# Row maxima sent through memory: as single values, or turned on VectorE and sent in 128-byte pieces

## The chip, the cores and the metric

The kernel runs on one core of one Trainium2 chip. The metric is the time of one execution on the device in microseconds (us), the slowest core's; here there is one. The core has TensorE (PE) for matmuls, VectorE (DVE), ScalarE (ACT) and GpSimd (POOL) for the rest, SyncE (SP) that only issues transfers, and 16 DMA engines that carry them. Each engine takes its instructions in the order in which they stand, and a transfer is issued by an instruction in some engine's order.

## The reference

Four batches of eight heads, 768 positions, 64 dimensions. Each query and key gets six hash bits (the signs of its products with six random vectors); a query sees only the keys of the same bucket. The attention's output goes through a feed-forward layer with a gate that is a convolution over three positions.

```python
q_bits = (np.einsum('bhsd,dk->bhsk', q, proj) > 0)
k_bits = (np.einsum('bhsd,dk->bhsk', k, proj) > 0)
mask = q_bucket[:, :, :, None] == k_bucket[:, :, None, :]
scores = scale * np.matmul(q, k.transpose(0, 1, 3, 2))
scores = np.where(mask, scores, -1000000000.0)
scores = scores - np.max(scores, axis=-1, keepdims=True)
attn = np.exp(scores)
attn = attn / (np.sum(attn, axis=-1, keepdims=True) + 1e-09)
x = np.matmul(attn, v)                  # heads joined: (4, 768, 512)
h = np.maximum(x @ w_in, 0.0)           # 512 -> 1024
gate = 1.0 / (1.0 + np.exp(-conv_out))  # conv_out: h over 3 positions
out = (h * gate) @ w_out                # 1024 -> 512
```

## The kernel before, in words

The order of the work is written out by hand; every engine runs its instructions as the code records them. Two heads make a pair: 16 pairs, four to a batch, and after every fourth pair the feed-forward layer of that batch.

Matmuls take operands that are split into a high and a low part. For a pair, Q and K stand with the dimensions on the partitions: tile q's first half (QA) has the high part in partitions 0 to 63, the hash bits in 64 to 95 as large numbers that make keys of another bucket lose, and **in partition 96 a row with each query's maximum**. The row of K that meets it is -1, so the score matmul (L290) subtracts the maximum, and ScalarE can take the exponential straight from the matmul's result (L293, tile p). Scores stand with the keys on the partitions, so the maximum has to be a row along the queries.

The maxima are made one pair ahead. `peak(t, h)` multiplies 128 queries (tile t of 6) of head h with all 768 keys (L246, tile m), and VectorE reduces that to one value per query (L249), a column of the tile `stat`, which has the 128 queries on the partitions. Such a column has to become a stretch of QA's row 96. For the first pair TensorE does that (`shift_now`). For the other 15 it goes through memory, on ScalarE's queue: `shift_away` writes columns of `stat` to a tile `top` in memory (L269), `shift_back` reads `top` as rows into QA's row 96 (L272). Each of the 15 pairs does it twice: for tiles 0 to 3 (eight columns, two heads) and for tiles 4 and 5 (four columns).

A pair takes six iterations, i = 0 to 5. Each has the scores and exponentials of two key tiles (L290, L291, L293), up to three `peak`s of the next pair, and the value matmuls (L301, tile v, eight a time) of the iteration before. i = 0 to 2 are the first 416 queries, 3 to 5 the other 352. The sums' additions (L316 on POOL, L314 on VectorE), the division (L334 to L345) and the output's split (L349, L353) follow. `shift_away` for tiles 0 to 3 stands in i = 4 behind the first exponential, its `shift_back` ahead of the exponentials of i = 5; for tiles 4 and 5 they stand in i = 0 and i = 1 of the pair that uses them.

Meanwhile the pair after next is prepared, on SyncE's queue: load R (L161, both heads' Q and K) and v (L165); hash R on TensorE (L174, in i = 3); turn the signs to bits on VectorE (L180); write the bits to memory (L183, far<-bits, 192 KB); make the high part on ScalarE (L188, hi) and the low part on POOL (L192, R); move hi and far into place (L198 to L201, each in an early and a late part); then hi and the low part into the second half of q and k (L207), and only then load the next R. SyncE's queue is in order too: k<-far (L199) holds all that stands behind it until far<-bits has landed.

In batch 0 the weights are also split into high and low parts, step by step, on VectorE, ScalarE and POOL (L90 to L112, tiles wu, wl, wi, wo).

Of the kernel before, what the change touches and what calls it, by code (L numbers as in the profile page):

```python
# [7 lines left out]
F32 = mybir.dt.float32  # L8
# [9 lines left out]
P = 128  # L18
NP = H // 2
NCK = S // P  # L20
# [24 lines left out]
def lsh_attention_conv_ffn(ctx, tc, qk, v, hw, w_in, conv_w, w_out, consts, ident_in, out):  # L45
    nc = tc.nc
    PSUM = bass.MemoryType.PSUM
    cp = ctx.enter_context(tc.tile_pool(name="const", bufs=1))
    wp = ctx.enter_context(tc.tile_pool(name="work", bufs=1))
# [4 lines left out]
    def ring(pool, bufs, shape, dtype, tag, name):  # L54

        k = turns[tag] = (turns.get(tag, -1) + 1) % bufs
        return pool.tile(shape, dtype, tag=f"{tag}{k}", name=name, bufs=1)
# [12 lines left out]
    dp = ctx.enter_context(tc.tile_pool(name="dram", bufs=1, space=bass.MemoryType.DRAM))  # L70
# [53 lines left out]
    def fetch(n):  # L124

        for src, name in blocks[:n]:
            raw = cp.tile([P, 2 * WC], I32, tag=f"w{name}", name=f"raw{name}")
            nc.sync.dma_start(raw, src)
            fetched.append((raw, name))
        del blocks[:n]  # L130

    def background(rate, stop):

        step[0] += 1
        if rate and len(fetched) > (2 if blocks else 0) and step[0] // rate > (step[0] - 1) // rate:
            splits.append(split_weight(*fetched.pop(0)))
        now = splits[:]
        while now:
            for g in now[:]:
                ended = next(g, None)  # L140
                if ended is None:
                    splits.remove(g)
                if ended is None or ended >= stop:
                    now.remove(g)


    class Pair:
# [94 lines left out]
        def peak(self, t, h):  # L242

            mp = ring(ps, 3, [P, 2, 512], F32, "S", f"m{self.nm}_{t}_{h}")[:, :, :HS + 2]
            for half in range(2):
                nc.tensor.matmul(mp[:, half], self.QA[:96, h, t * P:(t + 1) * P],  # L246
                                 self.K[0][:96, h, half * HS:(half + 1) * HS + 2], start=True, stop=True)
            c = self.column(t, h)
            nc.vector.tensor_reduce(self.stat[:, c:c + 1], mp, mybir.AxisListType.XY, ALU.max)  # L249
# [4 lines left out]
        def shift_now(self, t0, n):  # L254
# [7 lines left out]
            for h in range(2):  # L262
                nc.scalar.copy(self.QA[96:97, h, t0 * P:(t0 + n) * P], tp[96:97, h, :n * P])

        def shift_away(self, t0, n):
            c = self.column(t0, 0)
            k = turns["E"] = (turns.get("E", -1) + 1) % 4
            self.top = dp.tile([2 * n, P], F32, tag=f"top{k}", name=f"top{self.nm}_{t0}")
            nc.scalar.dma_start(self.top.rearrange("c p -> p c"), self.stat[:, c:c + 2 * n])  # L269

        def shift_back(self, t0, n):
            nc.scalar.dma_start(self.QA[96:97, :, t0 * P:(t0 + n) * P].bitcast(F32),  # L272
                                self.top.rearrange("(h t) p -> h (t p)", h=2).unsqueeze(0))


    class Block:
# [122 lines left out]
    def load_table(func):  # L399

        nc.scalar.activation(spare, cst[:, 3:4], func)
# [59 lines left out]
    first = pairs[0]  # L461
# [11 lines left out]
    def bring(n):  # L473

        if n < len(pairs):
            pairs[n].place_b()
        if n + 1 < len(pairs):
            pairs[n + 1].load()
        if n < len(pairs):
            pairs[n].load_v()  # L480
# [4 lines left out]
    for n, pr in enumerate(pairs):  # L485
        nxt, nx2 = (pairs[n + k] if n + k < len(pairs) else None for k in (1, 2))
        if nxt:
            units += [(nxt, t, h) for t in range(NCK) for h in range(2)]
        if n == 0 or pr.p:
            bring(n + 1)  # L490
        for i in range(6):
            places = (PEAKS if n else PEAKS_0)[i]

            def peak(place):
                if place in places and units:
                    u, t, h = units.pop(0)
                    u.peak(t, h)

            for bk in late:
                bk.divide()  # L500
                tail.append(bk)
            late = []
            ready, waiting = waiting, []
            blk = both[n][i // 3]
            if i == 5 and nxt:
                nxt.shift_back(0, 4)
            if i == 1 and n:
                pr.shift_back(4, 2)
            for k in range(2):
                c = 2 * (i % 3) + k  # L510
                if len(blk.pts) == c:
                    blk.scores(c)
                waiting.append((blk, c))
                if k == 0:
                    if i == 4 and nxt:
                        nxt.shift_away(0, 4)
                    if i == 0 and n:
                        pr.shift_away(4, 2)
                    peak(0)
                    for bk in tail:  # L520
                        bk.out_high()
            peak(1)
            for bk in tail:
                bk.out_low()
            tail = []
            for bk, c in ready:
                bk.values(c)
                if c <= DADD:
                    bk.add(c)
            if n == 0 and i == 2:  # L530
                first.shift_now(4, 2)
            for bk in summing:
                bk.sums()
                bk.invert()
            late, summing = summing, [bk for bk, c in ready if c == NCK - 1]
            background(RATE, 1)
            peak(2)
            if i == 5 and nx2:
                nx2.place_a(slice(0, EARLY_Q), slice(0, EARLY_K))
            for bk, c in ready:  # L540
                if c > DADD:
                    bk.add(c)
            if nx2:
                if i == HASH:
                    nx2.hash()
                    nx2.bits_up()
                    nx2.high()
                if i > HASH:
                    nx2.low(i - HASH - 1)
            if n or i:  # L550
                fetch(1)
            background(RATE, 1)
        if nx2:
            nx2.place_a(slice(EARLY_Q, S), slice(EARLY_K, S))
        if pr.p == NP - 1:
            bk, rest = both[n][1], waiting
            waiting = []
            load_table(AF.Sigmoid)
            bring(n + 2)

            def fill(i, tile):
                if i == 0:
                    for b2, c in rest:
                        b2.add(c)
                if i == 1:
                    for b2, c in rest:
                        b2.values(c)
                if i == 2:
                    bk.sums(tile[:, 0, :])
                    bk.invert()  # L570
                    bk.divide()
                if i == FLAG:
                    bk.out_high()
                    bk.out_low()

            def ahead():
                if nxt:
                    both[n + 1][0].scores(0)

            ffn(pr.b, [pairs[pr.b * NP + c].x for c in range(NCC)], fill, ahead)  # L580
# [42 lines left out]
```

## Time and profile before

| | |
|---|---|
| median of 3 runs | 990.1 us (987.84 to 996.34) |
| the profiled execution's own time | 990.33 us |
| its span, first to last instruction | 988.5 us |
| mean granted TensorE clock | 0.872 of full speed |
| busy, share of the span | PE 79%, DVE 56%, POOL 42%, ACT 36% |
| batches of attention, roughly | 0 to 206, 300 to 460, 533 to 694, 768 to 912 us |
| feed-forward layers, roughly | 206 to 300, 460 to 533, 694 to 768, 912 to 988 us |

Times in the profile are us from the span's start. A line such as "L293 ACT p<-s" names the line of the kernel, the engine, and the tiles written and read. "ACTq" and "SPq" are the queues of those engines, where transfers are issued. In brackets at an instruction's end stands how long its engine was idle before it, and what ended that.

### The profile page before, as it was taken

The page shows a single profiled execution, that of the slowest core. Times are in us where ns is not written, and L with a number is a line of the kernel's source. Part 1 is how long each engine was busy: PE and PEld are TensorE (multiplying, and loading weights), DVE is VectorE, ACT ScalarE, POOL GpSimd, SP SyncE. Part 2 cuts the span into 40 slices and gives each one's busy share as a digit, 9 for nine tenths or more (in the row PEclk, how much of TensorE's full clock was granted, in tenths as well). Part 3 has the DMA queues.
Part 4 walks back from the last instruction along what each step waited for, and adds up shares of the span by engine and source line. Part 5 has one row for each costly group of instructions (what it writes and reads, how often), then busy time and mean ns, then how long its engine had stood idle before and what let it go on. Part 6 is the DMA issues. An engine that isn't in the chain of part 4 may idle for free.

```text
span 988.5 us, 9984 instructions
## 1 busy us (share of the span) xinstructions
PE 784.7 (79%) x3552; PEld 547.5 (55%) x3552; DVE 550.4 (56%) x728; ACT 360.0 (36%) x582; POOL 410.4 (42%) x264
## 2 busy tenths in 40 slices
PE   6757575866896786787997877868999669678998
PEld 4433343445784443445896544534888445345896
DVE  4566676798862452645663535436665346363664
ACT  4324241444452232333543323322555323233553
POOL 5454646565423553533222534435122345334222
PEclk9878777797998897978999878879899889788999
DMA  3765757351005355364204163553500444600000
GB/s 102 199 117 170 126 160 115 89 109 47 0 32 33 51 120 99 69 137 79 80 32 32 14 112 75 117 95 77 145 0 32 33 59 112 114 2 0 1 32 33
DMA packets 57918, 75.48 MB, mean 76 GB/s; under 512 B 27872, under 2 KB 36334, under 8 KB 57868
## 3 DMA queue, kind: packets, MB, share of 16 engines
q1 hardware_dynamic: 33940, 74.60, 36.4%
q10 hardware_dynamic: 23928, 0.24, 1.2%
q8 instruction: 28, 0.46, 0.2%
q14 instruction: 22, 0.18, 0.1%
HBM read 29.71 MB, written 9.33 MB: 39 GB/s over the span
## 4 chain that ended last, share of the span: by engine, by line
PE 43%; DMA 34%; DVE 14%; ACT 4%; issue 3%; SPq 2%; ACTq 1%; DVEq 0%
DMA top<-stat 17%; PE o L389 11%; PE v L301 8%; DMA k<-far 8%; PE spot L364 7%; DMA far<-bits 5%; PE m L246 5%; PE h L364 4%; PE s L290 3%; DVE ht L373 3%; DVE stat L249 3%; PE s L291 3%; DMA q<-top 2%; PE sum L324 1%; DVE ps L314 1%
## 5 line engine op out<-in xcount | busy, mean ns | idle before, releaser
L293 ACT ACTIVATE p<-s 128x836 f32<-128x836 f32 (+1 forms) x192 | 152.6, 811 | 427.8 <-DMA top<-stat 214.3
L249 DVE TENSOR_REDUCE stat<-m 128x1 f32<-128x772 f32 x192 | 181.5, 953 | 175.6 <-PE m L246 174.4
L246 PE MATMUL m<-k,q 96*128 96x386 f32 x384 | 128.4, 419 | 137.7 <-ACT p L293 94.4
L316 POOL TENSOR_TENSOR ps<-ps,p 128x832 f32<-128x832 f32 (+1 forms) x92 | 157.7, 1714 | 187.2 <-ACT p L293 177.9
L246 PEld LDWEIGHTS m<-k,q 96*128 96x128 f32 x384 | 72.8, 219 | 204.2 <-ACT p L293 109.2
L290 PE MATMUL s<-q,k 97*128 97x418 f32 (+1 forms) x384 | 155.3, 405 | 29.8 <-DMA q<-top 19.3
L301 PE MATMUL v<-p,v 128*64 128x418 f32 (+1 forms) x768 | 173.0, 578 | 2.5 <-DVE bits L180 2.5
L381 POOL TENSOR_TENSOR g<-ht,g 128x384 fp32r<-128x384 f32 x64 | 69.3, 1083 | 220.4 <-ACT g L380 196.3
L373 DVE SCALAR_TENSOR_TENSOR ht<-ht,cw 128x384 f32<-128x384 f32 (+1 forms) x128 | 119.7, 935 | 56.6 <-ACT ht L371 53.3
L389 PE MATMUL o<-wo,g 128*128 128x512 f32 x576 | 145.2, 399 | 6.3 <-DVE r L334 6.3
L291 PE MATMUL s<-q,k 128*128 128x418 f32 (+1 forms) x384 | 145.4, 379 | 0.0
L389 PEld LDWEIGHTS o<-wo,g 128*128 128x128 f32 x576 | 108.7, 190 | 28.2 <-DVE r L334 6.6
L290 PEld LDWEIGHTS s<-q,k 97*128 97x128 f32 x384 | 84.5, 220 | 70.8 <-issue 25.3
L316 POOL TENSOR_TENSOR ps<-p,p 128x832 f32<-128x832 f32 (+1 forms) x32 | 58.5, 1828 | 123.4 <-ACT p L293 123.4
L364 PE MATMUL spot<-xh,wi 128*128 128x386 f32 x320 | 92.9, 352 | 11.6 <-ACT ht L369 11.5
L301 PEld LDWEIGHTS v<-p,v 128*64 128x64 f32 x768 | 52.9, 155 | 75.6 <-issue 69.0
L291 PEld LDWEIGHTS s<-q,k 128*128 128x128 f32 x384 | 84.7, 221 | 1.4
L353 DVE TENSOR_TENSOR xl<-r,xh 128x416 fp32r<-128x416 f32 (+1 forms) x32 | 34.6, 1081 | 73.1 <-ACT xh L349 73.1
L376 ACT ACTIVATE ht<-ht 128x384 f32<-128x384 f32 x64 | 33.6, 525 | 106.7 <-DVE ht L373 106.7
L192 POOL TENSOR_TENSOR R<-R,hi 128x768 fp32r<-128x768 f32 x30 | 66.0, 2202 | 14.1 <-PE hash L174 8.2
L364 PEld LDWEIGHTS spot<-xh,wi 128*128 128x128 f32 x320 | 61.1, 195 | 17.5 <-ACT ht L369 14.1
L364 PE MATMUL h<-xh,wi 128*128 128x386 f32 x192 | 56.7, 358 | 0.0
(83 smaller groups left out, 734.4 us busy)
## 6 DMA issues: line engine op xcount, KB each, us to landing
R<-in_qk SPq DMA_DIRECT2D x15, 768.0 KB
v<-in_v SPq DMA_DIRECT2D x16, 384.0 KB
k<-hi SPq DMA_DIRECT2D x16, 384.0 KB
q<-hi SPq DMA_DIRECT2D x16, 384.0 KB
out<-osb SPq DMA_DIRECT2D x24, 256.0 KB
q<-R SPq DMA_DIRECT2D x15, 384.0 KB
k<-R SPq DMA_DIRECT2D x15, 384.0 KB
rawi<-in_w_in SPq DMA_DIRECT2D x8, 512.0 KB
```

The source lines that it names most:

```text
L192: nc.gpsimd.tensor_tensor(R, R.bitcast(F32), self.hi[:, h].bitcast(F32), ALU.subtract)
L246: nc.tensor.matmul(mp[:, half], self.QA[:96, h, t * P:(t + 1) * P], self.K[0][:96, h, half * HS:(half + 1) * HS + 2], start=True, stop=True)
L249: nc.vector.tensor_reduce(self.stat[:, c:c + 1], mp, mybir.AxisListType.XY, ALU.max)
L290: nc.tensor.matmul(sp[:, h], pr.KA[:97, h, ks], pr.Q[0][:97, h, qs], start=True, stop=False)
L291: nc.tensor.matmul(sp[:, h], pr.KB[:, h, ks], pr.Q[1][:, h, qs], start=False, stop=True)
L293: nc.scalar.activation(self.pts[c], sp, AF.Exp, scale=SCALE)
L301: nc.tensor.matmul(self.av[h * D:(h + 1) * D], pr.v[:, c, h, :], self.pts[c][:, h], start=(c == 0), stop=(c == NCK - 1), tile_position=(0, ...
L316: eng.tensor_tensor(self.acc, first if c == 1 else self.acc, pt, ALU.add)
L364: nc.tensor.matmul(hp[:, :HW], w, x[:, c0:c0 + HW], start=(n == 0), stop=(n == 3 * NCC - 1))
L373: nc.vector.scalar_tensor_tensor(t[:, a:z], ht[:, o + k - 1 + a:o + k - 1 + z], cw[:, f, k:k + 1], t[:, a:z], ALU.mult, ALU.add)
L381: nc.gpsimd.tensor_tensor(g[:, 1, :], t, g[:, 0, :].bitcast(F32), ALU.subtract)
L389: nc.tensor.matmul(op, l, r, start=(f == 0 and n == 0), stop=(f == NFC - 1 and n == 2))
```

## The change

A new function `turn` transposes 32 columns of `stat` on VectorE, in 32 x 32 blocks: block a of the result `side` (partitions 32a to 32a + 31) holds in partition 32a + c the values of column c for the queries 32a to 32a + 31. It is called right behind the last `peak` that fills the columns. `shift_away` then writes `side` instead of `stat`: a tile of 32 rows of 128 values in memory, each written as four pieces of 32 values. `shift_back` reads the rows it needs. All 32 columns that are turned are written, also those that nobody reads.

```diff
+        def turn(self, t0):
+            c = self.column(t0, 0)
+            self.side = ring(wp, 2, [P, 32], F32, "side", f"side{self.nm}_{t0}")
+            nc.vector.transpose(self.side, self.stat[:, c:c + 32])
+
         def shift_away(self, t0, n):
-            c = self.column(t0, 0)
             k = turns["E"] = (turns.get("E", -1) + 1) % 4
-            self.top = dp.tile([2 * n, P], F32, tag=f"top{k}", name=f"top{self.nm}_{t0}")
-            nc.scalar.dma_start(self.top.rearrange("c p -> p c"), self.stat[:, c:c + 2 * n])
+            self.top = dp.tile([32, P], F32, tag=f"top{k}", name=f"top{self.nm}_{t0}")
+            nc.scalar.dma_start(self.top.rearrange("c (a q) -> a c q", a=4), self.side)
 
         def shift_back(self, t0, n):
             nc.scalar.dma_start(self.QA[96:97, :, t0 * P:(t0 + n) * P].bitcast(F32),
-                                self.top.rearrange("(h t) p -> h (t p)", h=2).unsqueeze(0))
+                                self.top[:2 * n].rearrange("(h t) p -> h (t p)", h=2).unsqueeze(0))
...
                     u, t, h = units.pop(0)
                     u.peak(t, h)
+                    if h and t in (3, NCK - 1) and u is not first:
+                        u.turn(t // 4 * 4)
```

The order on SyncE, POOL and TensorE is the same as before, and on ScalarE too. VectorE has 30 more instructions. Here is VectorE before, at i = 3 of the last pair of batch 0, where the last two maxima of tile 3 are reduced (m and stat are those of `peak`, ps the sums, bits the hash bits):

```order
L249 TENSOR_REDUCE stat_83<-m_0_3_0_1169 128x1
L98 TENSOR_SCALAR wlo_1108<-wuo_1107 128x512
L100 SCALAR_TENSOR_TENSOR wlo_1108<-rawo_645,wlo_1108 128x512
L249 TENSOR_REDUCE stat_83<-m_0_3_1_1180 128x1
L314 SCALAR_TENSOR_TENSOR ps_3_0_1090<-ps_3_0_1090,p_3_0_5_1129 128x832
L180 TENSOR_SCALAR bits_1_1190<-hash_1_1185,cst 128x384
```

And the same place with the change (the lines behind the new function have moved by four):

```order
L249 TENSOR_REDUCE stat_83<-m_0_3_0_1181 128x1
L98 TENSOR_SCALAR wlo_1120<-wuo_1119 128x512
L100 SCALAR_TENSOR_TENSOR wlo_1120<-rawo_651,wlo_1120 128x512
L249 TENSOR_REDUCE stat_83<-m_0_3_1_1192 128x1
L268 STREAM_TRANSPOSE side_0_0_1196<-stat_83 128x32
L318 SCALAR_TENSOR_TENSOR ps_3_0_1102<-ps_3_0_1102,p_3_0_5_1141 128x832
L180 TENSOR_SCALAR bits_1_1204<-hash_1_1199,cst 128x384
```

The transpose stands between the reduction and the addition to the sums; the hash bits, which SyncE's queue waits for, come two instructions behind it. ScalarE's order at i = 4 and 5 of the same pair, before:

```order
L293 ACTIVATE p_3_1_2_1207<-s_3_1_2_1202 128x2x352
L269 DMA top_0_0_1209<-stat_83 128x8x1
L293 ACTIVATE p_3_1_3_1216<-s_3_1_3_1211 128x2x352
L272 DMA q_0_75<-top_0_0_1209 1x2x512
L293 ACTIVATE p_3_1_4_1258<-s_3_1_4_1253 128x2x352
```

and with the change:

```order
L297 ACTIVATE p_3_1_2_1221<-s_3_1_2_1216 128x2x352
L273 DMA top_0_0_1223<-side_0_0_1196 4x32x32
L297 ACTIVATE p_3_1_3_1230<-s_3_1_3_1225 128x2x352
L276 DMA q_0_75<-top_0_0_1223 1x2x512
L297 ACTIVATE p_3_1_4_1272<-s_3_1_4_1267 128x2x352
```

Nothing has moved here; what the transfer to memory writes is 4 x 32 x 32 values where it was 128 x 8 x 1.

## Rows read from the trace of the kernel before

**Rows 1.** The page, section 4: the chain of work that ended last, by line, as shares of the span.

```profile
DMA top<-stat 17%; PE o L389 11%; PE v L301 8%; DMA k<-far 8%; PE spot L364 7%; DMA far<-bits 5%; PE m L246 5%; PE h L364 4%; PE s L290 3%; DVE ht L373 3%; DVE stat L249 3%; PE s L291 3%; DMA q<-top 2%; PE sum L324 1%; DVE ps L314 1%
```

**Rows 2.** From the list of who waited for whom: us in total, times, longest. Then the transfer's issues: count, shortest, median and longest issue in ns, first and last start in us.

```profile
ACT p L293 <- DMA top<-stat: 214.3, 24, 10.8
...
L269 ACTq DMA_DIRECT2D top<-stat x30: 361/366/415, 49.1 to 887.1; - x30
```

**Rows 3.** TensorE's timeline, 355 to 402 us, the value matmuls alone: start, us, instruction.

```profile
357.29 1.62 PE L301 MATMUL v<-p,v 128*64 128x418 f32 x8
...
361.73 1.62 PE L301 MATMUL v<-p,v 128*64 128x418 f32 x8
...
366.48 1.41 PE L301 MATMUL v<-p,v 128*64 128x352 f32 x8
...
370.95 1.41 PE L301 MATMUL v<-p,v 128*64 128x352 f32 x8
...
382.18 2.60 PE L301 MATMUL v<-p,v 128*64 128x352 f32 x8
...
390.52 2.17 PE L301 MATMUL v<-p,v 128*64 128x418 f32 x8
...
397.23 1.62 PE L301 MATMUL v<-p,v 128*64 128x418 f32 x8
```

**Rows 4.** Windows of the same pair: from and to, length, then busy us (instructions) of PE, weight loads, DVE, ACT and POOL, the granted clock, the DMA engines' share, GB/s.

```profile
357.30:371.00 13.70, 13.64 (x77) 8.03 (x76) 10.49 (x16) 5.35 (x8) 8.98 (x6) 1.00 0.42 109
371.00:390.50 19.50, 10.27 (x37) 6.00 (x36) 4.77 (x5) 3.58 (x5) 5.00 (x3) 0.74 0.54 87
390.50:397.20 6.70, 6.70 (x27) 3.84 (x26) 4.06 (x7) 2.78 (x4) 4.04 (x3) 0.75 0.54 118
```

**Rows 5.** ScalarE's timeline, 355 to 402 us: the transfers to memory (L269) and back (L272), and the exponential behind each transfer back.

```profile
365.67 0.36 ACTq L269 DMA_DIRECT2D top<-stat  x1
...
375.89 0.56 ACTq L272 DMA_DIRECT2D q<-top  x1
376.55 0.76 ACT L293 ACTIVATE p<-s 128x704 f32<-128x704 f32 x1 [9.49 <-DMA top<-stat]
...
380.98 0.37 ACTq L269 DMA_DIRECT2D top<-stat  x1
...
389.85 0.55 ACTq L272 DMA_DIRECT2D q<-top  x1
390.50 1.63 ACT L293 ACTIVATE p<-s 128x836 f32<-128x836 f32 x2 [7.29 <-DMA top<-stat]
```

**Rows 6.** Other transfers that write to memory. Two steps of the chain that ended last (start, us from issue to landing), and SyncE's wait at the program's end for the last output.

```profile
22.64 4.65 DMA far<-bits
...
560.51 11.43 DMA far<-bits
...
SPq L619 <- DMA out<-osb: 2.1, 1, 2.1
```

**Rows 7.** The DMA view. ScalarE's queue, q10, from 365 to 377 us and from 380.9 to 390 us: packets, MB, their time as a share of 16 engines; and SyncE's k<-hi beside far<-bits, in the stretch from 365 to 377 and in that from 22.6 to 27.3.

```profile
q10 hardware_dynamic: 1040, 0.00, 3.9%
...
q10 hardware_dynamic: 528, 0.00, 3.4%
...
k<-hi SPq DMA_DIRECT2D x1, 256.0 KB
...
k<-hi SPq DMA_DIRECT2D x1, 384.0 KB
```

**Rows 8.** VectorE's transposes from the groups by line and shape: count, busy us, mean ns of one, idle before.

```profile
L342 DVE STREAM_TRANSPOSE r<-rec 128x416 f32<-128x416 f32 x16 | 9.6, 597 | 0.0
L342 DVE STREAM_TRANSPOSE r<-rec 128x352 f32<-128x352 f32 x16 | 8.6, 537 | 0.2
```

**Rows 9.** SyncE's queue from 355 to 402 us (start, us of the issue), and TensorE's hash of two pairs.

```profile
363.84 0.85 PE L174 MATMUL hash<-R,hw_sb 128*32 128x384 f32 x8
...
366.40 0.58 SPq L183 DMA_DIRECT2D far<-bits  x1
367.09 0.61 SPq L198 DMA_DIRECT2D k<-hi  x1
377.90 0.81 SPq L199 DMA_DIRECT2D k<-far  x1
...
384.16 0.60 SPq L207 DMA_DIRECT2D k<-hi  x1
...
390.06 0.59 SPq L207 DMA_DIRECT2D k<-R  x1
395.56 0.38 SPq L161 DMA_DIRECT2D R<-in_qk  x1
...
403.76 0.85 PE L174 MATMUL hash<-R,hw_sb 128*32 128x384 f32 x8
```

**Rows 10.** Behind the feed-forward layer of batch 0: ScalarE's transfers, and the matmul at which TensorE stood.

```profile
300.25 0.36 ACTq L269 DMA_DIRECT2D top<-stat  x1
...
311.02 0.57 ACTq L272 DMA_DIRECT2D q<-top  x1
...
312.61 1.01 PE L246 MATMUL m<-k,q 96*128 96x386 f32 x2 [7.28 <-ACT p L293]
```

**Rows 11.** The chain that ended last, at the last pair of batches 1 and 2: start, us.

```profile
446.86 11.21 DMA top<-stat
...
681.88 10.28 DMA top<-stat
```

**Rows 12.** Window of batch 0 from its first transfer of maxima on, columns as in rows 4.

```profile
49.00:206.00 157.00, 106.00 (x452) 61.98 (x451) 111.15 (x138) 48.37 (x71) 88.70 (x52) 0.79 0.59 125
```

## The prediction

> **What bounds the kernel now.** I read the page first. On the chain that ended last the largest entry is no engine but a transfer, top<-stat, with 17% of the span, ahead of every matmul line [rows 1]. The list of waits says who stands still: ScalarE's exponentials (L293) lost 214.3 us in 24 waits, 10.8 us at the longest, put down to that transfer, and the program issues it 30 times [rows 2]. So it stalls ScalarE's queue nearly every time.
>
> Then I looked at one pair in the middle of a batch. The eight value matmuls (L301) of each iteration mark its pace [rows 3]. Four starts from 357.29 on are 4.44, 4.75 and 4.47 us apart; the next intervals are 11.23, 8.34 and 6.71. A pair thus takes 39.9 us, of which 13.7 are even pace and 26.3 are three iterations that would need 13.3. [...]
>
> ScalarE's timeline tells what the stall is [rows 5]. The transfer to memory is issued at 365.67; the transfer back (L272) can leave only when it has landed, at 375.89, 10.2 us later; it stands in ScalarE's queue ahead of the next exponential, which starts at 376.55. The second of the pair, with half the columns, is issued at 380.98 and holds the queue until 389.85, 8.9 us.
>
> **Why it takes so long.** The packets of that queue (q10, which ScalarE feeds) number 1040 and 528 in the two stretches, and fill 3.9% and 3.4% of the engines' time [rows 7]. So the time isn't reading; it is the writing of single values. Half the values take nearly the same time (8.9 against 10.2 us), and after the feed-forward layer the half-size one takes 10.8 [rows 10]. So the count of values alone doesn't set it; 512 single values cost about what 1024 do. Other writes to memory bound it. The last output transfer, long rows, is over 2.1 us after the program's end begins to wait for it [rows 6]. The hash bits, rows of 1536 bytes and 192 KB, land in 4.65 us at 22.64, where no such transfer runs, and in 11.43 us at 560.51, right behind one [rows 6]. So the single values also delay the transfer behind them, and with it SyncE's queue: k<-far waits for those bits from 366.40 to 377.90 [rows 9].
>
> **The change, part by part.** (1) 30 transposes on VectorE. The trace has transposes of 416 and 352 columns at 597 and 537 ns [rows 8]; the slope of 0.94 ns a column puts 32 columns at 0.24 us, bounds 0 and 0.54. VectorE is busy 10.49 of 13.70 us where it is busiest in a pair [rows 4], and the transfer is issued behind an exponential, so I cost the 30 x 0.24 = 7 us at nothing; uncovered, they add 7.
>
> (2) The transfer now has 128 pieces of 128 bytes. Landing: at least 2.1 us (the output row), at most what it takes now, 8.9 to 10.8. Between these I take 3.1: if pieces cost alike, 1040 packets took 10.2 - 2.1 = 8.1 us, so 128 take 1.0, plus 2.1. The nearest row, the bits with as many pieces twelve times as long, lies at 4.65; I keep 2.1 and 6.2 (below, rival A) for the range. The issue itself (0.36 us) stays.
>
> (3) What it frees. Between the issue behind the first exponential of an iteration and the transfer back at the next iteration's start lies about one iteration, 4.45 us. A landing of 3.1 fits, so the wait on ScalarE goes. The broken iterations then run at 4.45: 6.8 + 3.9 + 2.3 = 12.9 us per joint between two pairs at most, and a pair takes 27.0.
>
> (4) What is late next. SyncE's loop [rows 9]: bits issued (366.40), landed 4.65 later, seven issues from 377.90 to 384.16 and two more of about 0.65, 7.6 us; k<-R lands 5.5 after its issue (390.06 to 395.56); the next load of R takes at most until the next hash, 8.2 (395.56 to 403.76); hash to bits 2.56 (363.84 to 366.40). Sum 28.5, near 27.0; the load is likely done earlier. I take 28.0, so 12 us a joint, not 12.9.
>
> The sum against the profiled execution's 990.3 us (span 988.5; the median of the runs, 990.1, is the same):
> - nine joints inside batches 1 to 3: 9 x 12 = 108.
> - three first pairs behind a feed-forward layer: TensorE idle 7.28 us there [rows 10], 3 x 7.3 = 22.
> - the last transfer before the layer in batches 1 and 2: 11.2 and 10.3 us [rows 11] where 4.45 are free, 6.8 + 5.8 = 13.
> - batch 0, three joints and one last transfer: there VectorE also splits weights and is busy 111.15 of 157 us [rows 12]. At most the other 46 can go; in-order waits between engines stay, so two thirds, 30.
>
> Together 173: 990.3 - 173 = **817 us**. If every joint gives 12.9, batch 0 all of its 46 and the layers 24, it is 117 + 24 + 13 + 46 = 200, 790. The broken iterations also hold less matmul work: 10.27 and 6.70 us at clock 0.74 and 0.75 are 12.6 at full clock, not 13.3, worth another 6 to 8: 782 is the low end.
>
> [...] The rows show 4-byte pieces landing in 8.9 to 10.8 us and pieces of 1536 bytes in 4.65 [rows 5, 6]; nothing lies between. [...]
>
> **Rivals.**
> A. Few streams. The new pattern is 4 x 32 x 32, and if each outer step is one stream, 32 pieces follow one another. By the larger transfer on 16 engines (1040 packets, 65 each, in 8.1 us, 0.125 us a packet), 32 take 4.0 and the landing is 6.2. That is 1.8 us over the free 4.45 at either transfer, and the bits behind it come up to 4 us later: the loop of 28.5 becomes 32.5, a joint saves 7.4. 9 x 7.4 + 3 x 5.5 + 2 x 4.5 + 20 = 112 (each term less by the 2 us; batch 0 by a third), **878**. For it: the small pieces. Against: 65 and 33 packets a stream take nearly the same time, so the count in a stream has not set it so far.
>
> B. The bits stay late. If their 11.4 us come from the 256 KB transfer issued 0.69 us behind them [rows 7, 9] and not from the maxima, SyncE's loop is 28.5 + 6.8 = 35.3, a joint saves 4.6: 9 x 4.6 + 22 + 13 + 15 = 91, **899**. Against: at 22.64 a larger one of the same kind, 384 KB, lies beside them [rows 7], and they took 4.65.
>
> C. Slower. A piece of 128 bytes may cost far more than a value. If the 32 pieces of a stream cost over (10.3 - 2.1) / 32 = 0.26 us each, a landing is later than now (10.3 is the mean of the five shown [rows 5, 10, 11]). At 0.30 us it is 11.7, 1.4 later, 30 x 1.4 = 42, and with the 7 us of transposes in front **1039**. Against: 128 pieces of 1536 bytes landed in 4.65, under 0.08 us each even in four streams.
>
> D. The pieces don't merge. If each element still went alone there would be 4096 instead of 1024, 2.1 + 32 us a landing, far slower (over 1,600). The built program has 32 as its innermost size on both sides, against 1 before, so I give it almost nothing. That nothing changes because the landing stays at 9 to 10 us has a small chance too: **990**.
>
> **Chances.** Forecast 0.76 (own range 782 to 855), A 0.11, B 0.08, C and D together 0.03, unchanged 0.02. What a measurement of this kernel can tell from no change is about 1%, 10 us. Faster 0.95, same 0.02, slower 0.03. The range takes in the forecast's low end and rival A with some room: 782 to 890; outside are B, C, D, unchanged and the forecast's tails, under 2 in 10.
>
> **What would show it.** Right: in the profile after, the issue of top<-side and the transfer back lie 3 to 4.5 us apart; the row "ACT p <- DMA top" falls from 214 us to under 30; the bits land in about 5 us and k<-far leaves that early; value matmuls come every 4.5 us, a pair takes 27 to 29 us at a clock near 1.00; the queue's packets fall to about 130 a transfer. Wrong: landings of 6 us or more (A), bits at 11 us with short landings of the maxima (B), or TensorE waiting for k<-far or the hash at every joint for more than 2 us, which would mean that SyncE's loop, not ScalarE's queue, sets the pace and that the 1.0 us taken for it is too small.

## The result, and the profile after

The changed kernel takes 811.7 us (median of 4 runs, 809.63 to 812.83) where the kernel before takes 989.7 (987.84 to 996.34 in 4 runs): a ratio of 0.8187, 95% interval 0.8151 to 0.8223. The forecast was 817. The profiled execution took 809.63 us, with a span of 807.8 and a mean granted clock of 0.960.

First the page of the changed kernel, section 4, the chain that ended last by line:

```profile
PE o L393 13%; PE v L305 10%; PE spot L368 8%; DMA k<-R 6%; DVE stat L249 5%; PE s L294 5%; DVE ht L377 4%; PE m L246 4%; PE s L295 4%; DMA R<-in_qk 4%; PE h L368 4%; DMA far<-bits 2%; PE sum L328 1%; SPq L207 1%; DVE wuo L92 1%
```

The transfer of maxima, 17% of the chain before [rows 1], isn't among these lines any more; one landing of it, 4.81 us at 680.27, still is on the chain. What is left of transfers, k<-R, R and far<-bits, is SyncE's loop.

The waits of the changed kernel (us in total, times, longest), ScalarE's exponentials and SyncE's queue, and that of SyncE's queue in the kernel before:

```profile
ACT p L297 <- PE s L295: 175.9, 99, 10.5
...
SPq L199 <- DMA far<-bits: 51.1, 15, 3.9
```

```profile
SPq L199 <- DMA far<-bits: 140.7, 15, 10.3
```

Of the 214.3 us that the exponentials lost to the transfer [rows 2], 0.6 are put down to it now; a wait of 4.11 us behind the landing of 4.8 that is shown below is put down to TensorE's maxima. The exponentials wait for TensorE's scores instead, which is how it should be on an engine that isn't the bound. SyncE's wait for the bits, up to 10.3 us before, is 3.9 at the longest.

ScalarE's timeline of the changed kernel, 320 to 352 us, answers to [rows 5]:

```profile
324.13 0.55 ACTq L273 DMA_DIRECT2D top<-side  x1
...
328.96 0.59 ACTq L276 DMA_DIRECT2D q<-top  x1
...
333.71 0.55 ACTq L273 DMA_DIRECT2D top<-side  x1
...
335.82 0.58 ACTq L276 DMA_DIRECT2D q<-top  x1
```

From issue to transfer back it is 2.1 us where nothing stands in front. At 324.13 it is 4.8: 0.23 us earlier SyncE has issued the hash bits, as the next rows show. It is 4.8 or 4.9 in all four pairs of batches 1 to 3 in which the bits go out just before the first transfer of maxima, and 2.0 or 2.1 in the other seven. Three steps of the chain that ended last, in that stretch:

```profile
310.50 7.00 DMA k<-R
...
317.58 4.68 DMA R<-in_qk
...
323.90 4.64 DMA far<-bits
```

The bits land in 4.64 us, as they did in the kernel before only where no single values were on their way (4.65 against 11.43 in [rows 6]).

TensorE's timeline of the changed kernel, 293 to 358 us, the value matmuls and one hash, answers to [rows 3]:

```profile
297.32 1.40 PE L305 MATMUL v<-p,v 128*64 128x352 f32 x8 [1.58 <-DVE bits L180]
...
301.78 1.40 PE L305 MATMUL v<-p,v 128*64 128x352 f32 x8
...
305.41 1.41 PE L305 MATMUL v<-p,v 128*64 128x352 f32 x8
...
308.84 1.62 PE L305 MATMUL v<-p,v 128*64 128x418 f32 x8
...
314.11 1.62 PE L305 MATMUL v<-p,v 128*64 128x418 f32 x8
...
322.31 0.85 PE L174 MATMUL hash<-R,hw_sb 128*32 128x384 f32 x8 [1.58 <-DMA R<-in_qk]
```

The three iterations that took 11.2, 8.3 and 6.7 us take 3.6, 3.4 and 5.3 (from 301.78 to 314.11), and eight value matmuls take 1.40 to 1.62 us, where 2.60 and 2.17 stand in [rows 3]. Two idle times of 1.58 us are left: at 297.32 the value matmuls wait until VectorE has made the bits, at 322.31 the hash waits for the load of R. Windows of the changed kernel, columns as in [rows 4]: one pair, then the attention of batches 1 to 3, then batch 0 from its first transfer on:

```profile
300.00:326.60 26.60, 24.92 (x134) 15.12 (x133) 17.99 (x28) 11.96 (x16) 15.53 (x9) 1.00 0.61 148
...
278.50:386.90 108.40, 100.84 (x529) 61.46 (x528) 74.56 (x105) 46.77 (x63) 69.44 (x39) 1.00 0.50 123
...
458.00:564.00 106.00, 100.84 (x531) 61.55 (x529) 73.72 (x105) 46.89 (x63) 69.04 (x39) 1.00 0.50 126
...
635.10:732.40 97.30, 93.56 (x489) 57.00 (x488) 62.72 (x90) 43.10 (x59) 61.89 (x35) 1.00 0.34 82
...
50.37:182.00 131.63, 101.70 (x447) 56.48 (x446) 118.32 (x141) 47.00 (x69) 89.13 (x52) 0.87 0.57 153
```

TensorE is busy 24.92 of 26.60 us of a pair, at granted clock 1.00 where a joint had 0.74 and 0.75 [rows 4]. The three batches take 108, 106 and 97 us where they took 160, 161 and 144: 153 of the 181 us of span that went. Batch 0 with its feed-forward layer gave 22 (the first transfer of batch 1 is issued at 278.50 instead of 300.25), the other three layers together 6. In batch 0 VectorE is busy 118.32 of 131.63 us: it is the busiest engine there, and close to being the bound.

### The profile page after: what moved, and what is told of

The parts are those of the page before. It is cut to its first block, busy times and chain, and to the rows that moved or that the text cites. A ratio compares the mean times of both kernels' runs of the same rounds, so it can differ in the third digit from the quotient of the medians.

```text
span 807.8 us, 10032 instructions
## 1 busy us (share of the span) xinstructions
PE 724.2 (90%) x3552; PEld 512.4 (63%) x3552; DVE 562.9 (70%) x758; ACT 361.8 (45%) x582; POOL 404.9 (50%) x264
## 4 chain that ended last, share of the span: by engine, by line
PE 50%; DVE 23%; DMA 15%; issue 5%; ACT 4%; SPq 2%; POOL 1%; ACTq 0%; DVEq 0%
PE o L393 13%; PE v L305 10%; PE spot L368 8%; DMA k<-R 6%; DVE stat L249 5%; PE s L294 5%; DVE ht L377 4%; PE m L246 4%; PE s L295 4%; DMA R<-in_qk 4%; PE h L368 4%; DMA far<-bits 2%; PE sum L328 1%; SPq L207 1%; DVE wuo L92 1%
## 5 line engine op out<-in xcount | busy, mean ns | idle before, releaser
L305 PE MATMUL v<-p,v 128*64 128x418 f32 (+1 forms) x768 | 155.2, 527 | 13.9 <-DVE bits L180 13.9
L294 PE MATMUL s<-q,k 97*128 97x418 f32 (+1 forms) x384 | 141.1, 368 | 19.5 <-DVE stat L249 9.5
L295 PE MATMUL s<-q,k 128*128 128x418 f32 (+1 forms) x384 | 132.6, 345 | 0.0
L246 PE MATMUL m<-k,q 96*128 96x386 f32 x384 | 114.6, 384 | 12.9 <-DVE stat L249 5.9
L246 PEld LDWEIGHTS m<-k,q 96*128 96x128 f32 x384 | 66.2, 199 | 71.9 <-DVE stat L249 28.6
L294 PEld LDWEIGHTS s<-q,k 97*128 97x128 f32 x384 | 74.2, 193 | 55.3 <-DVE stat L249 20.8
L368 PE MATMUL spot<-xh,wi 128*128 128x386 f32 x320 | 92.5, 351 | 11.7 <-ACT ht L373 11.7
L295 PEld LDWEIGHTS s<-q,k 128*128 128x128 f32 x384 | 74.7, 194 | 0.7
L192 POOL TENSOR_TENSOR R<-R,hi 128x768 fp32r<-128x768 f32 x30 | 59.1, 1971 | 21.6 <-PE hash L174 13.8
L381 DVE TENSOR_TENSOR ht<-ht 128x384 f32<-128x384 f32 x64 | 36.0, 563 | 31.9 <-ACT ht L380 31.9
L368 PE MATMUL spot<-xl,wi 128*128 128x386 f32 x160 | 55.5, 347 | 0.0
```

The source lines that it names most:

```text
L192: nc.gpsimd.tensor_tensor(R, R.bitcast(F32), self.hi[:, h].bitcast(F32), ALU.subtract)
L294: nc.tensor.matmul(sp[:, h], pr.KA[:97, h, ks], pr.Q[0][:97, h, qs], start=True, stop=False)
L295: nc.tensor.matmul(sp[:, h], pr.KB[:, h, ks], pr.Q[1][:, h, qs], start=False, stop=True)
L305: nc.tensor.matmul(self.av[h * D:(h + 1) * D], pr.v[:, c, h, :], self.pts[c][:, h], start=(c == 0), stop=(c == NCK - 1), tile_position=(0, ...
L368: nc.tensor.matmul(hp[:, :HW], w, x[:, c0:c0 + HW], start=(n == 0), stop=(n == 3 * NCC - 1))
```

## The experiments

Three questions: is it the transposes, the transfers, or each of the two a pair; is it the hold of ScalarE or the delay of what else is on its way; and why are single values slow.

**One transfer at a time, and the transposes alone.** The first kernel turns only the eight columns of tiles 0 to 3, the second only the four of tiles 4 and 5 (the same edit with 4 for 0 and NCK - 1 for 3):

```diff
-            self.top = dp.tile([32, P], F32, tag=f"top{k}", name=f"top{self.nm}_{t0}")
-            nc.scalar.dma_start(self.top.rearrange("c (a q) -> a c q", a=4), self.side)
+            if t0 == 0:
+                self.top = dp.tile([32, P], F32, tag=f"top{k}", name=f"top{self.nm}_{t0}")
+                nc.scalar.dma_start(self.top.rearrange("c (a q) -> a c q", a=4), self.side)
+            else:
+                c = self.column(t0, 0)
+                self.top = dp.tile([2 * n, P], F32, tag=f"top{k}", name=f"top{self.nm}_{t0}")
+                nc.scalar.dma_start(self.top.rearrange("c p -> p c"), self.stat[:, c:c + 2 * n])
...
-                    if h and t in (3, NCK - 1) and u is not first:
+                    if h and t == 3 and u is not first:
```

> Only the eight columns of tiles 0 to 3 are turned; tiles 4 and 5 still go as 512 single values. Theory (each transfer's wait on ScalarE is a cost of its own, and the first one also delays the hash bits behind it): the first broken iteration of a joint goes, 6.8 of 12.9 us; 9 x 6.8 + 13 + some 14 in batch 0 = 88, so about 900 us (885 to 915), first landing 2 to 5 us, second still 8 to 11, hash bits 4.6 to 6 us. Rival (the two waits overlap with the same later one, so that the second swallows what the first gives): 940 or more.

> Only the four columns of tiles 4 and 5 are turned; tiles 0 to 3 still go as 1024 single values. Theory: the second broken iteration and the slow one after it go, 3.9 + 2.3 = 6.2 of 12.9 us; 9 x 6.2 + 22 + some 8 in batch 0 = 86, so about 905 us (890 to 920); the hash bits stay at 11 us, behind the first transfer. Rival (late hash bits take the place of the second wait, since k<-far then ends last): 930 or more, with TensorE waiting for k<-far at each joint.

Measured: 926.5 us (before 990.5; ratio 0.936, 0.930 to 0.942) and 897.3 (0.907, 0.901 to 0.913). SyncE's issues of the bits, one a pair, mark the pairs; shown are two issues with one between them, of the first kernel and then of the second:

```profile
320.77 0.59 SPq L183 DMA_DIRECT2D far<-bits  x1
...
391.34 0.59 SPq L183 DMA_DIRECT2D far<-bits  x1
```

```profile
304.10 0.59 SPq L183 DMA_DIRECT2D far<-bits  x1
...
374.16 0.59 SPq L183 DMA_DIRECT2D far<-bits  x1
```

Two pairs take 70.6 and 70.1 us, so one takes 35.3 and 35.0. By the same mark the changed kernel's seven pairs inside batches 1 to 3 take 26.1 to 28.9 us, 26.9 in the mean, and those of the kernel before 39.9 to 41.2, 40.6 in the mean. So each transfer of single values alone costs about 8 us a pair, and both together 13.7: the costs overlap. That is why the two savings, 64 and 93 us, are 157 together and the change gave 178. The first missed its expectation (900) by 26 us: I had given the second transfer 6.1 us of a joint, and alone it costs about 8.4. The second lies inside its range (890 to 920).

The transposes alone, with the single values sent as before:

```diff
+                    if h and t in (3, NCK - 1) and u is not first:
+                        u.turn(t // 4 * 4)
```

> The 30 transposes alone: VectorE turns the columns, and the single values are sent as before. Theory (they lie in VectorE's idle time): 990 us, within 3. Rival (they stand ahead of the addition and the hash bits and push the chain): 30 x 0.21 = 6 us or more, 996 and up.

Measured: 990.6 us in 10 runs beside 990.5, ratio 1.0027 (0.9984 to 1.0069). The profile of that kernel has them as

```profile
L268 DVE STREAM_TRANSPOSE side<-stat x30: 211/211/213, 49.0 to 886.7; 128x32 f32<-128x32 f32 x30
```

211 ns each (0.24 in the forecast), 6.3 us of VectorE's time. The medians agree to 0.1 us, so none of it is seen in the time; the interval reaches to 0.7%, or 6.8 us, so it doesn't by itself exclude the rival's 6.

**Hold or delay.** The changed kernel, with the old transfer beside the new one, into a tile that nobody reads:

```diff
+            c = self.column(t0, 0)
+            self.old = dp.tile([2 * n, P], F32, tag=f"old{k}", name=f"old{self.nm}_{t0}")
+            nc.scalar.dma_start(self.old.rearrange("c p -> p c"), self.stat[:, c:c + 2 * n])
```

> The changed kernel, and behind each transfer of turned maxima the old transfer of single values as well, to a tile in memory that nobody reads or waits for. Theory (the single values also hold up other transfers, not only ScalarE): the hash bits behind them land in 10 us or more instead of 4.7, SyncE's loop grows to about 35 us, and a joint takes 7 to 8 us more; 870 to 890 us. Rival (only ScalarE's wait counted): 812 to 820, hash bits at 5 us.

Measured: 951.3 us (ratio 0.961, 0.956 to 0.967), more than either theory said. Of the chain that ended last, 360 to 392 us:

```profile
367.32 10.87 DMA far<-bits
...
379.72 8.77 DMA q<-far
```

and ScalarE's transfers in the same pair:

```profile
377.09 0.49 ACTq L276 DMA_DIRECT2D old<-stat  x1
...
388.51 0.58 ACTq L279 DMA_DIRECT2D q<-top  x1
```

The bits are late as expected. But the transfer back also stands until 388.51, though its maxima were sent in the new way at 376.50: it leaves when q<-far lands (379.72 + 8.77 = 388.49). The profile puts the 10.65 us that ScalarE stands idle there down to that landing; why this transfer back waits for q<-far, no run shows. ScalarE's queue is held again all the same. So this run has the delay and part of the hold, and doesn't tell them apart. The next one has the old transfer only behind the first of a pair:

```diff
+            if t0 == 0:
+                self.old = dp.tile([2 * n, P], F32, tag=f"old{k}", name=f"old{self.nm}_{t0}")
+                nc.scalar.dma_start(self.old.rearrange("c p -> p c"), self.stat[:, :2 * n])
```

> As the run with the old transfers beside the new ones that nobody waits for, but only behind the first transfer of a pair (tiles 0 to 3, 1024 single values); the second stays as changed. It has the late hash bits and the late transfer back, and no hold at the second transfer. Theory (the late bits lengthen SyncE's loop): hash bits at 10 to 11 us, a pair 33 to 36 us, 870 to 900 us. Rival (the late bits have slack in SyncE's loop, and what counts is the hold of ScalarE at either transfer): a pair under 30 us, 835 or less.

Measured: 886.4 us (before 993.2; ratio 0.894, 0.883 to 0.905), inside the theory's range. SyncE's issues of the bits in that kernel, and two steps of its chain that ended last in that stretch:

```profile
306.35 0.59 SPq L183 DMA_DIRECT2D far<-bits  x1
...
340.57 0.58 SPq L183 DMA_DIRECT2D far<-bits  x1
...
377.93 0.59 SPq L183 DMA_DIRECT2D far<-bits  x1
...
410.42 0.58 SPq L183 DMA_DIRECT2D far<-bits  x1
```

```profile
305.95 9.15 DMA q<-top
...
341.45 9.04 DMA top<-side
```

Three pairs take 34.2, 37.4 and 32.5 us, 34.7 in the mean. That is near 35.3, SyncE's loop with late bits as rival B had added it up, but the bits, late though they are, don't stand on the chain here. What stands on it is the reading back of the maxima, which lands 9.15 us after its issue, and in the second pair the new transfer of maxima, which lands after 9.04 us and holds ScalarE as the old one did before the change. So the time came out in the theory's range by luck: its path isn't the one shown, and the run isn't free of holds. Of the seven pairs inside batches 1 to 3, five have no hold of 9 us or more and take 32.2 to 34.2 us, about 6 more than in the changed kernel. That is what single values cost by delaying other transfers: on the chain stands the reading back of the maxima in four of the five pairs (8.4 to 10.5 us), the bits in the fifth (10.53 us at 585.34). What late bits alone would cost stays open. The opposite, the hold without the small writes, has small transfers to and fro ahead of each transfer back:

```diff
+    probe = cp.tile([1, 16], F32, name="probe")
+    far_probe = dp.tile([1, 16], F32, name="far_probe")
...
         def shift_back(self, t0, n):
+            nc.scalar.dma_start(probe, self.top[0:1, 0:16])
+            for k in range(3 if t0 else 4):
+                src, dst = (far_probe, probe) if k % 2 else (probe, far_probe)
+                nc.scalar.dma_start(dst, src)
```

> The changed kernel, with ScalarE's queue held as long as before but without the many small writes: ahead of each transfer back stand four or five transfers of 64 bytes to and fro, each waiting for the one before. The transfer back then leaves 8 to 11 us behind the issue of the maxima. Theory (the hold of ScalarE and the delay of other transfers run side by side, and either alone makes most of a pair's 40 us): a pair takes 35 to 39 us, 930 to 975 us. Rival 1 (the delay of other transfers is all that counts): 812 to 840. Rival 2 (the hold alone was the whole cost): 985 to 1000.

Measured: 1014.8 us (before 990.2; ratio 1.024, 1.014 to 1.034), above every expectation. ScalarE's timeline of that kernel, one pair:

```profile
382.26 0.55 ACTq L275 DMA_DIRECT2D top<-side  x1
...
393.77 0.57 ACTq L282 DMA_DIRECT2D q<-top  x1
...
398.50 0.54 ACTq L275 DMA_DIRECT2D top<-side  x1
...
410.24 0.58 ACTq L282 DMA_DIRECT2D q<-top  x1
```

and two steps of its chain that ended last:

```profile
340.10 4.71 DMA far<-bits
...
384.64 4.74 DMA far<-bits
```

The holds are 11.5 and 11.7 us, 1.3 and 2.9 more than the 10.2 and 8.9 of [rows 5]; the bits land in 4.7; a pair takes 44.5 us. Less those 4.2 us it is 40.3, where the kernel before has 40.6 in the mean. This is an estimate: it takes a us more of hold for a us more of a pair. By it the hold alone makes the whole of the 13.7 us, the delay of other transfers alone about 6; they run side by side, and the change takes both away.

**Why single values are slow.** The old transfer beside the new one, and ScalarE held until it has landed, by reading two of its values back (`probe`). Then the same with 64, 512 and 16 bytes from value to value; for 64:

```diff
+    probe = cp.tile([1, 2], F32, name="probe")
...
+            self.old = dp.tile([2 * n, P, 16], F32, tag=f"old{k}", name=f"old{self.nm}_{t0}")
+            nc.scalar.dma_start(self.old.rearrange("c p z -> p c z")[:, :, 0:1], self.stat[:, c:c + 2 * n].unsqueeze(2))
...
         def shift_back(self, t0, n):
+            nc.scalar.dma_start(probe, self.old[0:1, 0:2, 0])
```

> As the one before (the old transfer of single values beside the new one, to a tile of its own), and ScalarE's queue waits for it as it did before the change, by reading two of its values back ahead of the transfer back. Both theories: the kernel before is back, 980 to 1005 us, 9 to 11 us from the issue of the single values to the probe. It is the measure for the next two.

> The same as the run before, but each single value goes to a place of its own, 64 bytes from the next. Theory 1 (single values are slow because many of them meet in the same stretch of memory): 3 to 5 us to the probe, 815 to 850 us. Theory 2 (each of the 1024 or 512 small writes costs its time, wherever it goes): 9 to 11 us, 980 to 1005.

> The same again with 512 bytes between the values, so that no two of them lie in one piece of 512 bytes. Theory 1: 3 to 5 us to the probe, 815 to 850 us, as with 64 bytes or below it where 64 was too near. Theory 2: 9 to 11 us, 980 to 1005.

> As the run with 64 bytes between the single values, but with 16: four values in each 64 bytes instead of one, or of sixteen as before the change. Theory (writes that meet in one stretch of 64 bytes wait for one another): a quarter of the way from 2.9 to 9 us for eight columns, 3.5 to 5.5 us from issue to probe, 825 to 870 us. Rival (the stretch that matters is longer than 64 bytes or the distance doesn't count gradually): 8 us or more, or as with 64 bytes, under 3.2.

Measured, one run each (before 993.4, for the last 990.2): 1024.2, 828.8, 832.5 and 845.1 us. ScalarE's timelines, from the transfer to the probe. Side by side in memory:

```profile
337.26 0.49 ACTq L277 DMA_DIRECT2D old<-stat  x1
346.32 0.24 ACTq L280 DMA_DIRECT2D probe<-old  x1
```

64 bytes apart:

```profile
352.72 0.50 ACTq L277 DMA_DIRECT2D old<-stat  x1
355.58 0.57 ACTq L280 DMA_DIRECT2D probe<-old  x1
...
364.53 0.62 ACTq L277 DMA_DIRECT2D old<-stat  x1
367.22 0.57 ACTq L280 DMA_DIRECT2D probe<-old  x1
```

512 bytes apart:

```profile
352.26 0.50 ACTq L277 DMA_DIRECT2D old<-stat  x1
354.90 0.57 ACTq L280 DMA_DIRECT2D probe<-old  x1
```

16 bytes apart:

```profile
359.83 0.49 ACTq L277 DMA_DIRECT2D old<-stat  x1
362.92 0.57 ACTq L280 DMA_DIRECT2D probe<-old  x1
...
389.26 0.50 ACTq L277 DMA_DIRECT2D old<-stat  x1
395.33 0.57 ACTq L280 DMA_DIRECT2D probe<-old  x1
```

The same number of 4-byte writes takes 9.1 us side by side, 2.9 and 2.7 with 64 bytes between, and hardly less, 2.6, with 512. Over the 30 transfers of each run the medians are 10.2, 2.7 and 2.8 us. So neither the count nor the size of the writes made them slow, but that they lie close together. That 512 values took as long as 1024 [rows 5, 10] fits this: as many lie in each stretch of memory. With 16 bytes between, four values in 64 bytes, it is 3.1 us where the bits weren't issued beside it, less than the 3.5 expected (3.4 is the median of 30), and 6.1 next to the hash bits, where 64 and 512 bytes apart take 5.3 to 5.9 too. So most of the cost has gone at 16 bytes; how it grows below that, and up to what distance closeness counts, stays open. The memory that the values cover grows with the distance, and no run tells the two apart. The first of the four is slower than the kernel before by more than the theory allowed; most likely the extra transfers and the probe hold ScalarE's queue too: in the pair shown it is 9.95 and 10.45 us from the issue of the new transfer to the transfer back (336.65 to 346.60, 353.43 to 363.88), beside 10.2 and 8.9 in [rows 5].

**What binds after the change.** SyncE's order turned round, so that R is free sooner:

```diff
-            for dst, src in ((QB[:64], hi[:64]), (KB[64:], hi[64:]), (QB[64:], lo[:64]), (KB[:64], lo[64:])):
+            for dst, src in ((QB[64:], lo[:64]), (KB[:64], lo[64:]), (QB[:64], hi[:64]), (KB[64:], hi[64:])):
```

> The changed kernel with one order turned round on SyncE: the two transfers that read R (its low part) go before the two that read the high part, so that the next load of R, which waits for them, can start earlier. Theory (SyncE's loop from hash bits to hash bits sets the pace after the change): the load is issued 3 to 5 us earlier, the hash's waits for it go, and up to 1.6 us a joint comes: 800 us (792 to 807). Rival (TensorE's and VectorE's own work sets the pace): 812 within 4.

Measured: 812.6 us (809.02 to 814.27, ratio to before 0.8176, 0.8148 to 0.8204): no difference from the change. The wait was taken away all the same. SyncE's wait ahead of the load of R in that kernel (69.9 us in 14 waits in the changed one):

```profile
SPq L161 <- DMA k<-R: 24.3, 14, 3.4
```

and its chain that ended last:

```profile
PE 62%; DVE 26%; issue 6%; ACT 3%; DMA 2%; SPq 0%; DVEq 0%; ACTq 0%
```

Transfers are 2% of it. So SyncE's loop was on the chain, but only just ahead of TensorE's and VectorE's own work, as the rival said.

**Few streams.** The turned maxima written as they stand, so that the write's outermost step is 128 instead of 4, and gathered on the way back:

```diff
-            self.top = dp.tile([32, P], F32, tag=f"top{k}", name=f"top{self.nm}_{t0}")
-            nc.scalar.dma_start(self.top.rearrange("c (a q) -> a c q", a=4), self.side)
+            self.top = dp.tile([P, 32], F32, tag=f"top{k}", name=f"top{self.nm}_{t0}")
+            nc.scalar.dma_start(self.top, self.side)
...
+            for h in range(2):
+                dst = self.QA[96:97, h, t0 * P:(t0 + n) * P].bitcast(F32).rearrange("o (t a q) -> o t a q", a=4, q=32)
+                src = self.top.rearrange("(a c) q -> c a q", a=4)[h * n:(h + 1) * n].unsqueeze(0)
+                nc.scalar.dma_start(dst, src)
```

> The turned maxima are written as they stand, 128 rows of 32 values one behind the other, and the transfer back gathers pieces of 128 bytes, one transfer for each head. Theory (the outer step of 4 had let few engines carry the write, which costs nothing where the transfer is alone, 2.0 us either way, but 2 to 3 us where it stands behind the hash bits): the landing next to the hash bits falls from 4.8 to about 2.5 us; the time stays, 812 within 6, since nothing waits for it any more. Rival (few streams cost time): 800 or less. Rival (gathering small pieces is slow): 820 and up.

Measured: 813.4 us (808.02 to 818.79; ratio 0.821, 0.806 to 0.836). Its transfers of the first kind:

```profile
353.24 0.32 ACTq L273 DMA_DIRECT2D top<-side  x1
...
354.70 1.30 ACTq L279 DMA_DIRECT2D q<-top  x2
```

1.5 us to the transfer back instead of 2.0 to 2.1; in the one pair with the bits just ahead it is 1.9 (382.75 to 384.64) instead of 4.8. As expected it changes no time, since nothing waits for it. The form of the write matters a little, not enough to be seen in the kernel; how many engines carry it in either form, no view shows.

## Why the prediction was right

By its own steps:

- **What bounds** held in both halves: ScalarE's wait vanished, and the hash bits land in 4.6 us. I had weighed the first as the cause and the second as what comes next. By the runs the hold alone keeps the whole of the joint, and the delay of other transfers alone some 6 of its 13.7 us; that the reading back of the maxima is among those delayed (9.15 us) I had not seen.
- **(1) The transposes**: 211 ns, nothing seen in the time, as forecast.
- **(2) The landing**: 3.1 us taken, 2.0 to 2.1 measured where nothing is ahead, the low bound of the output row, and 4.8 right behind the bits. Pricing each packet alike was wrong: 1024 single values took 9.1 us side by side and 2.9 with 64 bytes between them. The issue, taken as unchanged at 0.36 us, takes 0.55.
- **(3) and (4) The joint**: 12 us taken, 13.7 measured (26.9 against 40.6, the means of seven pairs). The 28.0 for SyncE's loop was the mis-sized term: R came 4.7 us after its issue, not the 8.2 that its row allowed at most, and with that loop shortened the time doesn't move (812.6 us). The low end's 12.6 us are an estimate from [rows 4], 10.27 x 0.74 + 6.70 x 0.75; eight value matmuls took 2.60 and 2.17 us in those two windows and 1.41 and 1.62 at clock 1.00. With first and last pairs, batches 1 to 3 gave 153 us where I had 108 + 22 + 13 = 143, and the layers behind them 6 where I had nothing.
- **Batch 0**: 30 taken, 22 measured with the layer behind it. VectorE's idle time did fall by over two thirds, from 46 to 13 us, but it is busy longer in that window, 118.32 us where it was 111.15 [rows 12]; why, no run shows. The misses cancel by luck: 173 forecast, 178 measured in the medians.
- **The size of the pieces**, 4 or 1536 bytes in [rows 5, 6] with nothing between, did not decide: pieces of 128 bytes land in 2.0 us, no later than the 2.1 that SyncE waits for rows of 2048 bytes, and 4-byte values 64 bytes apart in 2.7 to 2.9. The write with an outer step of 128 is 0.5 us faster than that with 4 (1.5 us, 2.0 to 2.1); that few engines carried the latter is not shown, and it costs the kernel nothing.
- **Rivals**: A fell with the landing of 2.1. B's premise fell in the change itself (bits at 4.6). Its sum, 35.3 us a pair, comes near the 34.7 of the run with late bits, but there the bits aren't what the chain waits for. C and D fell with the landing. Two sums are off by a little: A's landing is 2.1 + 4.0 = 6.1, not 6.2, and nine joints of 12.9 are 116, not 117; neither changes a conclusion.

## What to carry to other kernels

Look at how close together the small writes of one transfer land, not only at how many there are: the same 4-byte values took 9 to 10 us side by side and 2.7 to 2.9 with 64 bytes between. When a transfer is slow, look at what is issued just behind it on other queues (here the bits, 11.43 us instead of 4.65) as well as at the queue that waits for it; two such costs can run side by side, and then removing either alone shows less than its share (here the two transfers one at a time gave 64 and 93 us, both together 178). A transfer that stands in a compute engine's order, and waits for another, holds that engine's real work (ScalarE stood 9.49 us ahead of an exponential [rows 5]): allow it one iteration to land (4.45 us here, where the new landing takes 2.0 to 2.1), or put it elsewhere.

## What the runs showed of the hardware that I had not expected

4-byte writes side by side, sixteen to each 64 bytes, took 9 to 10 us, 512 of them as long as 1024, and 2.7 to 2.9 us when each had 64 bytes for itself. While they ran, a transfer of 192 KB issued behind them on another queue took 10.9 to 11.4 us instead of 4.6, and the reading back of 2 KB of maxima took 10.6 us (at 307.00 in the run with both old transfers) where it takes 2.04 when they have passed (at 528.97 in the run with one), and kept TensorE waiting as well (22.6 us in 9 waits in the latter run). Holds of ScalarE's queue of 11.5 and 11.7 us a pair, with hardly any traffic in them, cost as much as the slow writes themselves (1014.8 us beside 990.2).
